# Decay scores of 13 of 32 head pairs moved from TensorE into VectorE's second operand, by a table in DRAM

## The chip, the cores and the metric

One core of one Trainium2 chip runs the whole program. The metric is device time in microseconds (us) of one execution. Engines are called PE (TensorE; PEld is its weight loads), DVE (VectorE), ACT (ScalarE), POOL (GpSimd) and SP (SyncE, which here only issues DMAs).

## The reference

For each of 8 batches and 8 heads, 576 positions and head dimension 64:

```
scores = q @ k.T / sqrt(64)
cum    = cumsum(log(clip(f, 1e-4, 1)))            # one row of 576 per head
decay  = cum[:, None] - cum[None, :]
scores = where(causal, scores + decay, -1e9)      # then softmax over keys
x      = softmax(scores) @ v                      # 8 heads side by side: 512 channels
gate   = sigmoid(conv over 5 positions of x, per channel)
out    = ((x @ w_val) * gate) @ w_out
```

The term `cum[:, None]` is the same for a whole row of scores and drops out of the softmax; what a kernel has to add is `-cum` of the key's position.

## The kernel before, in words

The work is cut into 32 pairs of heads (pair i is heads 2g and 2g+1 of batch i // 4). Two heads of 64 fill the 128 partitions. The 576 queries are nine blocks of 64; block j needs keys 0 to 64 j + 63. For a pair:

- **Scores** (`plan_s`). Three groups (`SG`, index u) of blocks: (8),(7); then (6,0),(2,4); then (1,3),(5). Each group takes one to three PSUM banks, and PE runs 64x64 tiles on all four quarters of its array. `decay` (before: 20 bf16 matmuls for each pair) adds the decays: its weights are a column of `pk`, a one-hot pattern repeated 64 times by a stride of zero, which picks three rows of `st`, the decays of many pairs as a sum of three bf16 parts. `prod` (20 fp32 matmuls, which the trace shows as 40 records) adds q times k. `mm` at line 233 is the helper that issues every matmul except the warm-up (line 352), so rows on line 233 are told apart by their tiles: `st,pk` is a decay, `Xr` a product, `U,vt` the attention times v (PV), `xh,wall` and `xl,wall` the w_val product (Mv), `hh` and `hl` the w_out product (Mo).
- **Softmax.** For each block DVE runs one custom instruction (line 423, `red`) that adds `mk` (zeros and, in the last 64 columns, the causal mask) to the scores in PSUM, scales them and keeps the row minimum in `negm`; ACT takes the exponential (line 427) into `P`, DVE transposes 32x32 blocks (line 462) into `T`, ACT or POOL copies half of it to `U` (line 248) and four DMAs (`U<-T`, line 260) carry the rest. Reciprocals of the sums travel by `zd` and `zb` through DRAM.
- **PV** writes x; a 5-tap convolution on POOL, ACT and DVE makes `gate`; x is split in `xh` and `xl` for Mv. After four pairs a batch's Mv and Mo can run.

At the start, f is loaded in two tables of 128 rows (21 pairs and 11 pairs, each row repeated up to three times). `logs` clips and takes the log, `decays` makes the running sum (line 337, a scan on DVE), its reference (line 339), the scaled values (line 341, ACT) and the three bf16 parts (`st`, by three casts at line 248 and two subtractions at line 345 in turn). Pair 0's products are issued ahead of its decays, since the decays come late. The weights w_val and w_out are decoded from 64-bit floats by lines 655 to 711 among the first pairs.

The order on every engine is fixed: each piece of work is a node of `Plan`, and `ORDER`, a compressed table of numbers, gives the sequence, the engine and the PSUM bank of each node. All DMAs go through SP's queue, one after another, but for the first two.

Of the kernel before, what the change touches and what calls it, by code (L numbers as in the profile page):

```python
# [793 lines left out]
```

## Time and profile before

| | us |
|---|---|
| median of three runs (439.27 to 442.82) | 439.31 |
| the profiled execution | 440.2 |
| its span, first to last instruction | 438.5 |
| PE busy in the span | 417.3 |
| DVE, ACT, POOL busy | 376.0, 335.5, 286.3 |

The span is 1.7 us shorter than the execution's own time; what lies around it is start and end of the program. All durations below are of this one execution, 0.9 us above the median. A group of PE rows is busy from the first start to the last end of its overlapping matmuls, so the cost of one kind of matmul is read from start to start: when the first of them begins, and when the next kind begins.

### The profile page before, as it was taken

The numbers are of one execution on the slowest core, as the hardware profiler recorded it, in microseconds if no ns is written. First come the engines' busy times: TensorE is split into PE (matmuls) and PEld (weight loads), VectorE is DVE, ScalarE is ACT, GpSimd is POOL, SyncE is SP. The second block draws the span as 40 slices with busy tenths as digits, with TensorE's granted clock in tenths as the row PEclk, the third lists the DMA queues.
The fourth block names the chain that finished last, engine by engine and source line by source line (L and its number), as shares of the span: only waits on it lengthen the run. The fifth ranks groups of instructions, "written<-read, shape, count | busy, mean of one in ns | idle before, by whom it ended". The sixth has DMA issues, their size and how long they took to land.

```text
span 438.5 us, 16745 instructions
## 1 busy us (share of the span) xinstructions
PE 417.3 (95%) x6640; PEld 356.5 (81%) x6640; DVE 376.0 (86%) x1045; ACT 335.5 (77%) x834; POOL 286.3 (65%) x296
## 2 busy tenths in 40 slices
PE   6768999999999999999999999899999999899996
PEld 5535788888898888898889789688889789799985
DVE  5999899899899898989989999598989879896840
ACT  5988899889779978877877888678778869682321
POOL 6576776687769686796367598769866864742200
PEclk9699999999999999999999999999999999999999
DMA  8679968976987886868678859886887757862112
GB/s 316 229 215 254 241 168 233 236 231 171 242 238 190 218 228 175 233 162 252 180 196 213 232 144 227 199 221 183 256 238 187 210 164 198 228 173 59 49 72 96
DMA packets 74847, 87.23 MB, mean 199 GB/s; under 512 B 48145, under 2 KB 48145, under 8 KB 74769
## 3 DMA queue, kind: packets, MB, share of 16 engines
q1 hardware_dynamic: 74480, 85.57, 70.9%
q8 instruction: 52, 0.85, 0.8%
q10 hardware_dynamic: 288, 0.59, 0.4%
q14 instruction: 27, 0.21, 0.2%
HBM read 52.29 MB, written 10.26 MB: 143 GB/s over the span
## 4 chain that ended last, share of the span: by engine, by line
PE 84%; DVE 6%; DMA 5%; issue 3%; SPq 1%; ACT 1%; POOL 0%; DVEq 0%; ACTq 0%; POOLq 0%
PE banks L233 84%; DVE banks L423 2%; DMA U<-T 2%; DVE T L462 2%; DMA sl<-in_w_out_dram 1%; DMA sh<-in_w_val_dram 1%; SPq L260 1%; DVE gate L345 0%; DVE negm L423 0%; DVE h L595 0%; DVE st L248 0%; DVE x L337 0%; POOL wall L711 0%; ACT ot L636 0%; DMA vt<-in_v_dram 0%
## 5 line engine op out<-in xcount | busy, mean ns | idle before, releaser
L427 ACT ACTIVATE P<-banks,negm 128x512 f32<-128x512 f32 (+8 forms) x288 | 149.6, 528 | 39.9 <-DVE negm L423 29.5
L423 DVE CUSTOM_DVE_ANT_0 banks<-banks,mk 128x512 f32<-128x512 f32 (+8 forms) x288 | 134.8, 506 | 16.3 <-PE banks L233 12.5
L564 POOL TENSOR_TENSOR gate<-gate,tm 128x576 f32<-128x576 f32 x77 | 109.5, 1424 | 46.8 <-DVE tm L255 11.0
L462 DVE STREAM_TRANSPOSE T<-P 128x1024 f32<-128x1024 f32 (+2 forms) x96 | 110.9, 1166 | 7.9 <-DMA U<-T 3.0
L233 PE MATMUL banks<-xh,wall 128*128 128x288 f32 x512 | 108.3, 298 | 0.0
L233 PE MATMUL banks<-Xr 64*64 64x288 f32 (+8 forms) x1280 | 104.2, 412 | 4.0 <-issue 2.8
L233 PEld LDWEIGHTS banks<-U,vt 64*64 64x64 f32 x3456 | 89.6, 133 | 6.8 <-ACT P L427 1.6
L233 PE MATMUL banks<-U,vt 64*64 64x128 f32 (+1 forms) x3456 | 91.0, 253 | 2.5 <-ACT P L427 1.0
L233 PE MATMUL banks<-wall,hh 128*128 128x512 f32 x288 | 90.5, 395 | 0.0
L233 PEld LDWEIGHTS banks<-xh,wall 128*128 128x128 f32 x512 | 83.6, 188 | 3.9 <-issue 0.9
L233 PEld LDWEIGHTS banks<-Xr 64*64 64x64 f32 x1280 | 65.0, 135 | 18.5 <-issue 9.4
L233 PE MATMUL banks<-xl,wall 128*128 128x288 f32 x256 | 75.5, 295 | 0.0
L248 ACT COPY U<-T 128x1440 f32<-128x1440 f32 x44 | 61.2, 1396 | 6.2 <-PE banks L233 3.2
L233 PEld LDWEIGHTS banks<-wall,hh 128*128 128x128 f32 x288 | 52.3, 188 | 12.0 <-issue 0.8
L427 ACT ACTIVATION_READ_ACCUMULATOR P<-banks,negm 128x1 f32 x288 | 58.4, 203 | 0.0
L233 PE MATMUL banks<-st,pk 64*64 64x256 bf16 (+8 forms) x640 | 47.8, 293 | 9.6 <-ACT P L427 6.1
L233 PE MATMUL banks<-wall,hl 128*128 128x512 f32 x144 | 56.2, 390 | 0.0
L233 PEld LDWEIGHTS banks<-xl,wall 128*128 128x128 f32 x256 | 48.1, 188 | 0.5
L233 PEld LDWEIGHTS <-pk 64*64 64x64 bf16 x640 | 27.7, 107 | 25.3 <-issue 20.4
L255 POOL TENSOR_SCALAR tm<-x,cw 128x576 f32<-128x576 f32 x36 | 27.7, 770 | 19.9 <-DVE gate L562 16.9
L423 DVE DVE_READ_ACCUMULATOR2_ANT negm<- 128x1 f32 x288 | 40.1, 139 | 0.0
L609 POOL TENSOR_TENSOR hl<-h,hh 128x576 fp32r<-128x576 f32 (+2 forms) x34 | 35.6, 1063 | 6.5 <-ACT tm L253 2.6
(103 smaller groups left out, 471.8 us busy)
## 6 DMA issues: line engine op xcount, KB each, us to landing
U<-T SPq DMA_DIRECT2D x128, 180.0 KB, 4.0
Xr<-in_x_dram SPq DMA_DIRECT2D x63, 288.0 KB, 5.0
vt<-in_v_dram SPq DMA_DIRECT2D x32, 320.0 KB, 5.0
out_dram<-ot SPq DMA_DIRECT2D x36, 256.0 KB, 3.6
vt<-in_v_dram SPq DMA_DIRECT2D x32, 256.0 KB, 5.5
zb<-zd SPq DMA_DIRECT2D x64, 80.0 KB, 4.0
zb<-zd SPq DMA_DIRECT2D x64, 64.0 KB, 3.6
sh<-in_w_val_dram SPq DMA_DIRECT2D x2, 512.0 KB
```

The costliest lines, as they stand in the source:

```text
L233: nc.tensor.matmul(out, lhsT=lhsT, rhs=rhs, start=start, stop=stop)
L248: (eng.copy if eng is nc.scalar else eng.tensor_copy)(out=out, in_=in_)
L255: eng.tensor_scalar(out=out, in0=in_, scalar1=col, scalar2=0.0, op0=ALU.mult, op1=ALU.add)
L260: lambda e: (nc.sync if e == "SP" else nc.scalar).dma_start(out=out, in_=in_), reads, writes, dma=span)
L423: nc.vector.tensor_tensor_reduce(out=sl, in0=sl, in1=mk[:, S - ext:], op0=ALU.add, op1=ALU.min, scale=-0.125, scalar=3.0e38, accum_out=neg ...
L427: nc.scalar.activation(out=dst, in_=bank(key)[:, a0:a0 + ext], func=AF.Exp, bias=negm[r][:, col], scale=-1.0, accum_out=zs[r][:, col])
L462: nc.vector.transpose(out=bass.AP(Tt.tensor, Tt.offset + 32 * FB[js[0]], [pitch, (32, nk), (CW, 2), (1, 32)]), in_=Pt[u])
L564: eng.tensor_tensor(out=gt, in0=gt, in1=to, op=ALU.add)
L609: eng.tensor_tensor(out=hl[jj][:, y:y + x1 - x0], in0=h2[jj % 2][:, x0:x1], in1=hh[jj][:, y:y + x1 - x0].bitcast(F32), op=ALU.subtract)
```

## The change

For 13 pairs, the odd ones from 7 to 31 (`TP`), PE runs no decay matmuls. The values of `-8 cum` are stored to DRAM (`lnf`), copied there into a table `tab` with every row eight times (three DMAs), and for each of the 13 pairs two DMAs of 128 x 576 floats bring the pair's rows, each to 64 partitions, into `dec` (two buffers). DVE's score instruction takes `dec` in place of `mk` as its second operand. The causal mask, which `mk` held, is then added on PE by 12 small bf16 matmuls a pair: an identity times a triangle, 64 or twice 64 columns each, behind the products.

Pair 0 takes its decays by fp32 matmuls straight from the scan's result (`cum`, with a one-hot column `p1` of -8), without the bf16 split. There is one f table in place of two (each pair once, and the first 16 pairs twice more), one log, one scan; the split runs for pairs 1 to 15 at the start and for 16 to 31 later, from `lnf`. The clearing of `mk` may go to DVE. `ORDER` is new.

```
-NS = (21, 11)
+NF = 16
+TP = tuple(range(7, 32, 2))
...
+        if i in TP:
+            for y in range(2):
+                load("dec", 1.4, i - 0.4 + 0.02 * y, dec[TP.index(i) % 2][:, y], bass.AP(tab.tensor, tab.offset + (24 * i + 8 * y) * S, [(S, 16), (0, 8), (1, S)]),
+                     [("tab", k) for k in range(3)], [("dec", TP.index(i) % 2, y)])
...
+    pool("start", 0.9, z + 3.27, mk_eyes, (), [("eyes",)])
+    any_("zero", {"POOL": 1.5, "DVE": 0.4}, z + 0.1, lambda eng: eng.memset(mk, 0.0), (), [("mk",)])
...
+                pick, row = (pk[hs, h, i:i + 1], st_) if i else (p1[hs], cum)
+                mm(bank(keys[y])[ps, at:at + e - a], pick.to_broadcast([D, D]), row[hs, a:e], start and fresh, last and stop)
...
+            def mask(h, half, item, start, stop, keys=keys):
+                y, js = item[:2]
+                hs, ps = slice(D * h, D * h + D), slice(D * half, D * half + D)
+                rhs = eyes[hs, 1]
+                to = bank(keys[y])[ps, (224 if js[0] == 8 else 0) + D * js[0]:]
+                gap = [(D * js[1] + D, 2)] if len(js) == 2 else []
+                mm(bass.AP(to.tensor, to.offset, [to.ap[0], *gap, (1, D)]), eyes[hs, 0],
+                   bass.AP(rhs.tensor, rhs.offset, [rhs.ap[0], *([(0, 2)] if gap else []), (1, D)]), False, stop)
...
-            if i:
-                pe("S", dur, p, lambda run=run, decay=decay, prod=prod: run((decay, prod)), ops + tab, keys, mode=1)
+            if late:
+                pe("S", (1.01, 0.9, 0.7)[u], p, lambda run=run, prod=prod, mask=mask: run((prod, mask)), ops + marks, keys, mode=1)
+            elif i:
+                pe("S", dur, p, lambda run=run, decay=decay, prod=prod: run((decay, prod)), ops + marks, keys, mode=1)
             else:
-                pe("S", dur, p, lambda run=run, prod=prod: run((prod,)), ops, keys, mode=1)
-                pe("Sd", 0.3, p, lambda run=run, decay=decay: run((lambda h, half, x, start: decay(h, half, x, False),)), tab, keys, mode=1)
+                pe("S", dur, p, lambda run=run, prod=prod: run((prod,), final=False), ops, keys, mode=1)
+                pe("Sd", (1.1, 1.0, 0.75)[u], p, lambda run=run, decay=decay: run((decay,), first=False), marks, keys, mode=1)
...
+                    in1 = dec[TP.index(i) % 2][:, y, 0:ext] if late else mk[:, S - ext:]
...
-                        nc.vector.tensor_tensor_reduce(out=sl, in0=sl, in1=mk[:, S - ext:], op0=ALU.add, op1=ALU.min, scale=-0.125,
+                        nc.vector.tensor_tensor_reduce(out=sl, in0=sl, in1=in1, op0=ALU.add, op1=ALU.min, scale=-0.125,
...
+        if not i:
+            load("lnf", 0.4, z + 1, lnf, val, kv, [("lnf",)], hold=0.48)
+            split(0, val, kv, z + 0.3)
+            for k in range(3):
+                load("tab", 1.6, z + 2 + 0.1 * k, bass.AP(tab.tensor, tab.offset + 8 * k * S, [(24 * S, NP), (S, 8), (1, S)]),
+                     bass.AP(lnf.tensor, lnf.offset + (0, D, 0)[k] * S, [(S, NP), (0, 8), (1, S)]), [("lnf",)], [("tab", k)])
```

In the rows below, numbers after a name tell its buffers apart (`Xr_76` and `Xr_80` both hold q and k of pair 7). On PE, the first scores of pair 7, first group. Before, the end of the decays and then the products:

```order
L233 LDWEIGHTS pk
L233 MATMUL banks<-st_70,pk 64x288
L233 LDWEIGHTS pk
L233 MATMUL banks<-st_70,pk 64x288
L233 MATMUL banks<-Xr_76 64x512 x2
L233 MATMUL banks<-Xr_76 64x288 x4
L233 LDWEIGHTS pk
L233 MATMUL banks<-st_70,pk 64x448
```

And now, the same group:

```order
L239 MATMUL banks<-Xr_80 64x288 x2
L239 MATMUL banks<-Xr_80 64x512 x2
L239 MATMUL banks<-Xr_80 64x288 x2
L239 LDWEIGHTS eyes
L239 MATMUL banks<-eyes 64x64
L239 LDWEIGHTS eyes
L239 MATMUL banks<-eyes 64x64
```

The six decays of up to 512 columns ahead of the products are gone, and four masks of 64 columns stand behind them.

On DVE, the start: from the scan to the first score instruction (ISA, with `banks` and `negm`). Before:

```order
L337 SCALAR_TENSOR_TENSOR x_100<-one,gate 128x576
L339 TENSOR_SCALAR ref_124<-x_100 128x1
L325 TENSOR_SCALAR tm<-tm 128x576
L248 CAST st_70<-gate 128x576
L345 SCALAR_TENSOR_TENSOR gate<-st_70,sel,gate 128x576
L248 CAST st_70<-gate 128x576
L345 SCALAR_TENSOR_TENSOR gate<-st_70,sel,gate 128x576
L248 CAST st_70<-gate 128x576
L703 TENSOR_SCALAR sh<-sh 128x512
L697 TENSOR_SCALAR sl<-sl 128x512
L703 TENSOR_SCALAR sl<-sl 128x512
L423 ISA banks,negm_89<-banks,mk 128x512
```

Now, from the operation ahead of the scan (the diagonal matrices of the first convolution, which POOL made before):

```order
L569 TENSOR_TENSOR tm<-ident,cw 128x640
L352 SCALAR_TENSOR_TENSOR x_104<-one,gate 128x576
L354 TENSOR_SCALAR ref<-x_104 128x1
L730 TENSOR_SCALAR sl<-sl 128x512
L736 TENSOR_SCALAR sl<-sl 128x512
L254 CAST st_70<-gate 128x576
L730 TENSOR_SCALAR sh<-sh 128x512
L736 TENSOR_SCALAR sh<-sh 128x512
L456 ISA banks,negm_93<-banks,mk 128x192
L456 ISA negm_93 128x1
L456 ISA banks,negm_93<-banks,mk 128x320
```

Two casts and both subtractions no longer stand ahead of pair 0's scores; seven score instructions of pair 0 are now ahead of the first subtraction, and the last cast of the split is on ACT, behind six exponentials of pair 0.

On SP, the DMAs behind the reciprocals (`zd_66`) of pair 4. Before:

```order
L260 DMA zd_66<-zt_95 4x32x32
L260 DMA zb_98<-zd_69 64x5x64 x2
L260 DMA zb_98<-zd_69 64x4x64 x2
L260 DMA U_84<-T_82 32x1440
L260 DMA Xr_76<-in_x_dram 128x576
L260 DMA zb_97<-zd_66 64x5x64
```

Now:

```order
L266 DMA zd_66<-zt_99 4x32x32
L266 DMA U_88<-T_86 32x1440
L266 DMA Xr_80<-in_x_dram 128x576
L266 DMA dec_73<-tab 128x1x576
L266 DMA zb_101<-zd_66 64x5x64 x2
L266 DMA ot<-in_w_out_dram 128x1024
```

A `dec` load, which pair 7's scores will need, has come between pair 4's transfers.

## Rows read from the trace of the kernel before

**Rows 1.** The page: busy engines, and the chain that ended last by engine.

```profile
PE 417.3 (95%) x6640; PEld 356.5 (81%) x6640; DVE 376.0 (86%) x1045; ACT 335.5 (77%) x834; POOL 286.3 (65%) x296
PE 84%; DVE 6%; DMA 5%; issue 3%; SPq 1%; ACT 1%; POOL 0%; DVEq 0%; ACTq 0%; POOLq 0%
```

**Rows 2.** Busy time by stretch: stretch, length, engines (x instructions), granted clock, DMA share, GB/s.

```profile
0.00:45.00 45.00, 31.20 (x421) 22.80 (x424) 39.30 (x121) 36.54 (x95) 29.15 (x56) 0.92 0.79 251
45.00:400.00 355.00, 351.31 (x6000) 303.38 (x5996) 317.12 (x886) 288.53 (x721) 254.25 (x238) 1.00 0.77 206
```

**Rows 3.** Timeline of PE, middle of the run: start, length, what, xcount.

```profile
188.53 0.36 PE L233 MATMUL banks<-st,pk 64*64 64x128 bf16 x6
188.72 0.81 PE L233 MATMUL banks<-Xr 64*64 64x128 f32 x12
189.37 0.41 PE L233 MATMUL banks<-st,pk 64*64 64x512 bf16 x6
189.59 1.16 PE L233 MATMUL banks<-Xr 64*64 64x512 f32 x12
...
197.81 0.46 PE L233 MATMUL banks<-st,pk 64*64 64x192 bf16 x7
198.03 0.57 PE L233 MATMUL banks<-Xr 64*64 64x192 f32 x3
```

**Rows 4.** Timeline of PE: two decays of 64 columns, and the next matmul.

```profile
193.32 0.19 PE L233 MATMUL banks<-st,pk 64*64 64x64 bf16 x2
193.35 0.57 PE L233 MATMUL banks<-Xr 64*64 64x448 f32 x4
```

**Rows 5.** Timeline of PE at the start, with the idle time ahead.

```profile
7.10 2.70 PE L233 MATMUL banks<-Xr 64*64 64x128 f32 x40 [1.16 <-DMA Xr<-in_x_dram]
12.47 0.81 PE L233 MATMUL banks<-st,pk 64*64 64x288 bf16 x20 [2.67 <-DVE st L248]
...
14.96 0.31 PE L233 MATMUL banks<-st,pk 64*64 64x128 bf16 x2 [0.62 <-ACT P L427]
```

**Rows 6.** Timeline of DVE at the start.

```profile
6.20 0.73 DVE L697 TENSOR_SCALAR sh<-sh 128x512 int32<-128x512 int32 x1 [0.72 <-DMA sh<-in_w_val_dram]
6.86 1.38 DVE L337 TENSOR_TENSOR_SCAN x<-one,gate 128x576 f32<-128x576 f32 x1
...
8.34 0.45 DVE L325 TENSOR_SCALAR tm<-tm 128x576 f32<-128x576 f32 x1
9.26 0.46 DVE L248 CAST st<-gate 128x576 bf16<-128x576 f32 x1 [0.47 <-ACT gate L341]
9.76 0.82 DVE L345 SCALAR_TENSOR_TENSOR gate<-st,sel,gate 128x576 f32<-128x576 bf16 x1
...
12.34 0.43 DVE L703 TENSOR_SCALAR sh<-sh 128x512 int32<-128x512 int32 x1
...
13.34 0.69 DVE L423 CUSTOM_DVE_ANT_0 banks<-banks,mk 128x512 f32<-128x512 f32 x1
```

**Rows 7.** Busy time by stretch at the start, columns as in rows 2.

```profile
13.20:20.10 6.90, 6.03 (x60) 4.47 (x58) 6.83 (x24) 6.72 (x21) 5.38 (x7) 0.51 0.70 236
```

**Rows 8.** DVE groups by line (the page, and with forms apart): xcount, busy, mean ns, idle before.

```profile
L423 DVE CUSTOM_DVE_ANT_0 banks<-banks,mk 128x512 f32<-128x512 f32 (+8 forms) x288 | 134.8, 506 | 16.3 <-PE banks L233 12.5
...
L528 DVE TENSOR_TENSOR xl<-x,xh 128x576 fp32r<-128x576 f32 x9 | 6.6, 753 | 0.3 <-ACT xh L248 0.2
```

**Rows 9.** DMA: SP's queue (packets, MB, share of 16 engines); one issue group's KB and landing.

```profile
q1 hardware_dynamic: 74480, 85.57, 70.9%
...
Xr<-in_x_dram SPq DMA_DIRECT2D x63, 288.0 KB, 5.0
```

**Rows 10.** The tile U: who waited for it (us, times), and its DMAs' time to landing.

```profile
PEld banks L233: 1.1, 2
PE banks L233: 0.7, 1
...
DMA to landing us min/median/max: 2.5/4.0/5.4
```

More of the change, by code (lines that the diff above doesn't have):

```diff
@@ L179, in tile_decay_attention_gated_mlp @@
     pk = const.tile([P, 2, NP], BF16, name="pk")
+    p1 = const.tile([P, 1], F32, name="p1")
     Xr = tiles(XB, [P, XW], F32, "Xr")
@@ L284, in mk_ident @@
                                 compare_op=ALU.is_equal, fill=0.0)
-    ref = [const.tile([P, 1], F32, name=f"ref{n}") for n in range(2)]
-    work = ((gate[2], x32[1][:, T0:], gate[0]), (tm[0], tm[1], tm[1]))
-    kws = (([("gate", 2)], [("x", 1, n) for n in range(3)], [("gate", 0)]), ([("tm", 0)], [("tm", 1)], [("tm", 1)]))
-    def load_f(n):
-        load("start", 0.75, z - 1 + n, work[n][0], f[n], (), kws[n][0], early=n == 0)
-    load_f(0)
+    ref = const.tile([P, 1], F32, name="ref")
+    ft, cum, val = gate[2], x32[1][:, T0:], gate[0]
+    kf, kc, kv = [("gate", 2)], [("x", 1, n) for n in range(3)], [("gate", 0)]
+    load("start", 0.75, z - 1, ft, f, (), kf, early=True)
     pool("start", 0.51, z, mk_ident, (), [("ident",)])
@@ L333, in decays, with mk_eyes @@
-    def decays(n):
-        (ft, cum, val), (kf, kc, kv) = work[n], kws[n]
-        p = z if n == 0 else NS[0] - 6.0
-        st_, ks = sts[n], [("st", n)]
-        dve("st0", 1.36, p, lambda: nc.vector.tensor_tensor_scan(out=cum, data0=one.to_broadcast([P, S]), data1=ft, initial=0.0, op0=ALU.mult, op1=ALU.add),
-            [*kf, ("one",)], kc)
-        dve("st0", 0.15, p, lambda: nc.vector.tensor_scalar(out=ref[n], in0=cum[:, S // 2:S // 2 + 1], scalar1=8.0, scalar2=0.0, op0=ALU.mult, op1=ALU.add),
-            kc, [("ref", n)])
-        act("st0", 0.76, p, lambda: nc.scalar.activation(out=val, in_=cum, func=AF.Identity, scale=-8.0, bias=ref[n]), [*kc, ("ref", n)], kv)
+    def mk_eyes():
+        nc.gpsimd.memset(eyes, 0.0)
+        for h in range(2):
+            for n, (op, fill) in enumerate(((ALU.not_equal, 1.0), (ALU.is_ge, -BIG))):
+                half = eyes[D * h:D * h + D, n]
+                nc.gpsimd.affine_select(out=half, in_=half, pattern=[[-1, D]], base=0, channel_multiplier=1, compare_op=op, fill=fill)
@@ L342, in decays, with split @@
+    act("st0", 0.76, z, lambda: nc.scalar.activation(out=val, in_=cum, func=AF.Identity, scale=-8.0, bias=ref), [*kc, ("ref",)], kv)
+    def split(n, val, kv, p):
+        st_, ks = sts[n], [("st", n)]
         for k in range(3):
@@ L717, in tile_decay_attention_gated_mlp @@
     for i in range(NP):
-        if i == NS[0] - 6:
-            load("lnf", 0.4, i, tm[0], lnf, [("lnf",)], kws[1][0], hold=0.48)
-            decays(1)
+        if i == NF - 6:
+            vb, kb = tm[0], [("tm", 0)]
+            for h in range(2):
+                load("lnf", 0.3, i, vb[D * h:D * h + D], bass.AP(lnf.tensor, lnf.offset + (D * h + NF) * S, [(0, 4), (S, NF), (1, S)]),
+                     [("lnf",)], kb, hold=0.48)
+            split(1, vb, kb, i)
         if i:
```

204 lines of the change are left out of this document (105 added, 99 removed).

## The prediction

> **What bounds the kernel now.** I read the page's busy line and chain first, then busy time by stretch, then the timelines of PE and DVE, then the DMA views. PE is busy 417.3 of 438.5 us and holds 84% of the chain [rows 1]. By stretch [rows 2] there are three parts. From 45 to 400 us PE is busy 351.31 of 355 us, so only 3.7 us are idle there; DVE has 317.12 (89%) and ACT 288.53 (81%). A microsecond of work taken from PE there shortens the run, unless DVE cannot feed PE that much sooner. From 0 to 45 us PE has 31.20 busy and 13.8 idle, while DVE is busy 39.30: DVE sets the pace of the start, since it has to bring the first four pairs through softmax, with the weights' decoding between them, before PE's other work exists. After 400 us only Mv and Mo of the last batches are left, which the change does not touch.
>
> **The decays taken from PE.** Each pair has 20 decay matmuls in three groups. From the start of a group's decays to the start of its products [rows 3]: 188.53 to 188.72 is 0.19 us, 189.37 to 189.59 is 0.22, 197.81 to 198.03 is 0.22. That is 0.63 us a pair, and the three groups have 5,760 columns together.
>
> In their place come 12 masks with 1,152 columns in all (six matmuls of 64 and six of 128). The trace has no masks. From below, by columns alone, they would take 1,152/5,760 of 0.63, that is 0.13 us. From above, if each cost as much as a decay of average size (0.63/20 = 0.032 us), 0.38 us. The nearest row is the pair of 64-column decays that start at 193.32, with the next matmul at 193.35 [rows 4]: 0.015 us each, so 12 take 0.18 us; I take 0.20, since half of them are twice as wide. So a pair saves 0.43 us (0.25 to 0.50), and 13 pairs save 5.6 us (3.3 to 6.5). It all lies on the path: the 13 pairs run between about 100 and 390 us, where PE has next to no idle time.
>
> The Trainium skill, page "TensorE: Matmul & The Clock Gate", section "Wait — 56ns, not 53.3ns?", speaks against part of this: start to start never drops below about 25 ns, however few columns. By that rule the masks would take 12 x 0.025 = 0.30 us and the 13 pairs would save 4.3 us; the two decays of rows 4, on different quarters of the array, came at 0.015 us each, which disagrees, so I keep the row.
>
> DVE's score instruction reads `dec` instead of `mk`: two operands of the same size and type from the same places. I take zero. It could only cost by waiting for the load, which is the last term.
>
> **The start.** Pair 0's decays wait today for the split: the products end at 9.80, and PE idles 2.67 us until the third cast is done [rows 5]. The split is three casts of 0.46 and two subtractions of 0.82 [rows 6], 3.0 us. Now pair 0's decays need the scan alone. As fp32 matmuls of the products' shapes they should take what those took, 2.70 us instead of 0.81 [rows 5]. The first group can start when the scan is done, about 8.3, or when PE is through with the products ahead of it, and it needs under 1.1 us (8 of 20 matmuls). So PE is ready with the first scores near 9.3 to 9.9.
>
> DVE then decides. Ahead of its scan now stand a clearing of `mk` and the diagonal (640 columns). Neither is in the trace on DVE; the nearest row is 0.753 us for 576 columns of a two-operand operation [rows 8], and the two together cost between 0.7 and 1.3 us. The wait of 0.72 us for the weights just ahead of the scan's neighbour [rows 6] no longer stands there and hides most of it. The scan therefore starts where it did, give or take 0.5 us. After it come the reference, four integer operations (the three ahead of the first score instruction take from 12.34 to 13.34, 0.33 each [rows 6]) and one cast: 1.4 + 0.2 + 1.3 + 0.5, with about half a microsecond of waiting for ACT's scaled values. The first score instruction starts near 10.5 instead of 13.34.
>
> That is not 2.8 us of gain. The other subtractions and casts move behind it, and pair 1 needs them. Two subtractions and one cast (2.1 us) plus eight score instructions (0.506 us on average [rows 8], 4 us) lie ahead of the last cast, which is now on ACT: pair 1's decays start near 16.6 where they started at 14.96 [rows 5]. There is a new wait as well: `val` is stored to `lnf` first, and the subtraction overwrites it, so it waits for that DMA. An `Xr` load of the same 288 KB takes 5.0 us to land [rows 9]; issued at about 9, it ends at 14, just when the subtraction's turn comes (10.5 plus 3.5 us for seven score instructions). Behind it on DVE stand the last two score instructions of pair 0 and its transposes. What is left is DVE's sum: out go a clip and a cast (0.45 and 0.46), and 1.2 us of waiting (0.72 and 0.47 in rows 6) is filled; in come 0.7 to 1.3 us. I take 1.0 us off the start. The bounds are 3.0 (all that the first score comes sooner is kept) and a loss of 2.0 (pair 1 is 1.6 us late, nothing is won back, and its first products follow later still).
>
> **The added DMA traffic.** SP's queue moved 85.57 MB in 70.9% of 438.5 us of all 16 engines, 3.63 us for each MB [rows 9]. 26 `dec` loads are 7.67 MB and take 27.8 us; three table copies of 0.59 MB take 6.4. One 288 KB load of f goes. Between 100 and 400 us that raises the DMA share of 0.77 [rows 2] by 0.09 to 0.86. PE waited for `U` 1.8 us in the whole run, in three waits, at a landing time of 4.0 us [rows 10], so most landings have room today. If landings stretch by about a tenth, a few more waits appear: I charge 0.8 us (0 to 10; the upper end is the last rival). SP issues 20 more DMAs of about half a microsecond each, over 300 us; its queue is not full.
>
> **Sum.** 440.2 for the profiled execution, minus 5.6, minus 1.0, plus 0.8, is 434.4. The median lies 0.9 below that execution, so I forecast 433.5 us.
>
> **The rivals.** One: *DVE gives half of it back.* From 45 to 400 us DVE is at 89%, and to do the same work in 5.6 us less it must reach 90.7%. For this speaks that PE's few waits are already on softmax results; against it, that DVE itself waits for PE. If half of the 5.6 returns as PE idle time and the start gives nothing, the time is 440.2 - 2.8 + 0.8 - 0.9 = 437.3.
>
> Two: *the start gets a second slow stretch.* PE's granted clock was half (1.2 instead of 2.4 GHz) from about 13.2 to 20.1 us [rows 7], after PE had idled 2.67 us up to 12.47 [rows 5]. Now it is busy there and idles later, from about 13.5 to 16.6, so the slow stretch may come when there is more to do. A slow stretch of 6.9 us costs at most half of it, 3.4 us, and today's cost nothing visible because DVE was busy throughout (6.83 of 6.90 [rows 7]). With 2.0 of that on the path and the 1.0 of the start lost: 433.5 + 1.0 + 2.0 = 436.5.
>
> Three: *the masks or the start do better.* Masks by columns alone and the whole 3.0 us of the start: 440.2 - 6.5 - 3.0 + 0 - 0.9 = 429.8.
>
> Four, on the other side: *the loads come in the way of `U`.* The DMA engines near nine tenths busy let the landing of `U<-T` grow from 4.0 us past what PV has as room. From the point where each of the 25 pairs from 7 on loses 0.27 us to it, the gain is gone (6.6/25). At 0.5 us for each, 12.5 us are lost, and the time is 440.2 - 6.6 + 12.5 - 0.9 = 445.2. For it speaks the share of 0.79 at the start [rows 2], which the changed kernel would exceed; against it, that PE waited only three times for `U`.
>
> **How the numbers follow.** The forecast has 0.58, with its own range of 431 to 436.5; rival one 0.15, two 0.07, three 0.10, four 0.10. A measurement of this kernel can tell about 1% from no change, 4.4 us, so "faster" is below 434.9. The forecast falls there in three cases of four (0.44), rival three always (0.10), the rest hardly (0.01): 0.55. Slower than 443.7 is rival four: 0.10. The rest, 0.35, is within 1%. The range from 429 to 440.5 leaves out most of rival four and little else.
>
> **What the profile of the changed kernel would show.** If right: PE busy near 412 us, a late pair's masks in 0.2 us from the first of them to the next kind, PE's idle time between 45 and 400 still under 6 us, the first score instruction on DVE between 10 and 11 us, PE's waits for `U` a few microseconds at most and DVE never long on `dec`. If wrong: PE's busy time down as said but its idle time up, with `DMA U<-T` as the releaser (rival four) or DVE's score instructions (rival one); a granted clock of one half later than 20 us (rival two); or masks at 0.3 us and more.

## The result, and the profile after

The changed kernel takes 443.64 us (median of 20 runs), the kernel before 440.55 in the same comparison: a ratio of 1.0056, interval 1.0032 to 1.0080. By the ratio it is slower by 2.5 us; 433.5 us was forecast, and 443.64 lies above the range that was given. The ratio leaves out the four of the changed kernel's runs that lie over 1.5% above its fastest one; the medians of all runs are 3.1 us apart. The profiled execution has a span of 440.7 us against 438.5.

The page of the changed kernel, busy engines and chain by engine [rows 1], then SP's queue [rows 9]:

```profile
PE 415.7 (94%) x6556; PEld 355.4 (81%) x6556; DVE 376.1 (85%) x1036; ACT 335.8 (76%) x840; POOL 284.6 (65%) x298
PE 55%; DMA 20%; DVE 10%; SPq 7%; ACT 3%; issue 3%; POOL 0%; DVEq 0%; ACTq 0%; POOLq 0%
q1 hardware_dynamic: 79032, 95.01, 80.6%
```

PE has only 1.6 us less to do, and its part of the chain has fallen from 84% to 55%: DMA and SP's queue together rise from 6% to 27%. A chain whose share moves from the busiest engine to the transfers says that the engine has begun to wait, even where its busy time fell.

Busy time by stretch, changed kernel [rows 2]; the last two are the stretches of half clock [rows 7]:

```profile
0.00:45.00 45.00, 33.82 (x427) 26.00 (x428) 37.84 (x116) 36.77 (x92) 23.41 (x57) 0.89 0.86 257
45.00:400.00 355.00, 344.89 (x5737) 296.37 (x5736) 315.27 (x876) 288.33 (x730) 256.46 (x238) 1.00 0.87 229
17.10:20.50 3.40, 3.40 (x36) 2.56 (x30) 3.40 (x6) 2.96 (x10) 2.30 (x7) 0.50 0.99 350
30.70:37.60 6.90, 5.47 (x122) 5.47 (x122) 4.35 (x19) 6.30 (x19) 3.84 (x3) 0.51 1.02 312
```

In the middle PE is now idle 355 - 344.89 = 10.1 us; it was 3.7. The work taken from PE has gone into waiting there. The DMA share went from 0.77 to 0.87, close to the 0.86 that was forecast from 100 us on.

Timeline of PE, changed kernel: masks of two late pairs and the matmul that follows them (start, length, what, xcount) [rows 3, 4]:

```profile
132.03 0.36 PE L239 MATMUL banks<-eyes 64*64 64x64 bf16 x4
132.32 0.40 PE L239 MATMUL banks<-xh,wall 128*128 128x288 f32 x1
...
183.30 0.26 PE L239 MATMUL banks<-eyes 64*64 64x128 bf16 x4
183.36 2.90 PE L239 MATMUL banks<-U,vt 64*64 64x128 f32 x106
...
186.96 0.20 PE L239 MATMUL banks<-eyes 64*64 64x64 bf16 x2
186.99 0.52 PE L239 MATMUL banks<-Xr 64*64 64x384 f32 x2
```

Ahead of other 64x64 tiles a mask takes 0.015 us (0.06/4 and 0.03/2), as the two decays of rows 4 did. Ahead of a 128x128 matmul four masks take 0.29 us, and the last of them about half of that (0.145 us, median of 14 such places in this trace). This should not be booked on the masks: in e12, which has none, the last product ahead of a 128x128 matmul is charged 0.31 us (median of 26).

Timeline of PE, then of DVE, at the start of the changed kernel [rows 5, 6]:

```profile
9.48 1.17 PE L239 MATMUL banks<-Xr 64*64 64x288 f32 x12
10.37 1.25 PE L239 MATMUL banks<-x,p 64*64 64x512 f32 x12
...
14.81 0.66 PE L368 MATMUL banks<-ident 128*128 128x128 f32 x4 [2.61 <-ACT P L460]
16.83 0.36 PE L239 MATMUL banks<-st,pk 64*64 64x128 bf16 x6 [1.36 <-ACT st L254]
```

```profile
6.44 1.35 DVE L352 TENSOR_TENSOR_SCAN x<-one,gate 128x576 f32<-128x576 f32 x1
...
9.97 0.35 DVE L456 CUSTOM_DVE_ANT_0 banks<-banks,mk 128x192 f32<-128x192 f32 x1
...
13.35 0.82 DVE L363 SCALAR_TENSOR_TENSOR gate<-st,sel,gate 128x576 f32<-128x576 bf16 x1 [0.33 <-DMA lnf<-gate]
```

The first score instruction starts at 9.97 (13.34 before), pair 1's decays at 16.83 (14.96 before). A lead of 3.4 us has become a lag of 1.9 within seven microseconds: the split now stands behind pair 0's scores. Pair 0's fp32 decays (`x,p`) took 1.54 us from 7.94 and 1.17 us from 10.37 to the next kind, 2.7 us as forecast, where the bf16 decays took 0.75 (12.47 to 13.22).

DVE's score instructions by operand, changed kernel [rows 8]:

```profile
L456 DVE CUSTOM_DVE_ANT_0 banks<-banks,mk 128x128 f32<-128x128 f32 (+8 forms) x171 | 80.1, 505 | 6.4 <-PE banks L239 4.9
L456 DVE CUSTOM_DVE_ANT_0 banks<-banks,dec 128x128 f32<-128x128 f32 (+8 forms) x117 | 55.2, 504 | 10.1 <-PE banks L239 6.5
```

504 ns from `dec`, 505 from `mk`: the other operand costs nothing. Most of the idle time ahead of either ends with PE, and no wait of DVE for a `dec` load is listed.

Waits for DMAs, changed kernel (who <- whom: us, times, longest) [rows 10], the last line from SP's own queue; then two places in PE's timeline; then a stretch of the chain that ended last (start, us, what):

```profile
DVE x L552 <- DMA zb<-zd: 6.9, 5, 2.4
PE banks L239 <- DMA zb<-zd: 2.0, 1, 2.0
PE banks L239 <- DMA Xr<-in_x_dram: 1.7, 2, 1.4
PE banks L239 <- DMA U<-T: 1.4, 1, 1.4
SPq L266 <- DMA dec<-tab: 5.4, 7, 1.2
```

```profile
32.16 5.08 PE L239 MATMUL banks<-U,vt 64*64 64x128 f32 x105 [1.43 <-DMA U<-T]
...
92.56 2.77 PE L239 MATMUL banks<-U,vt 64*64 64x128 f32 x106 [2.02 <-DMA zb<-zd]
```

```profile
81.92 0.22 DVE zt L473
82.14 0.02 issue
82.16 5.89 DMA zd<-zt
88.05 0.02 issue
88.07 0.02 SPq L266
88.09 0.03 issue
88.11 4.46 DMA zb<-zd
92.58 7.61 PE banks L239 x121
```

The reciprocals of a pair go out to DRAM (`zd`, 16 KB) and come back (`zb`), two DMAs in a row. Here they take 10.4 us, and PE idles 2.02 us ahead of PV at 92.56. PE's one wait for `U`, on which the forecast kept its eye, ends at 32.16, before the first `dec` load is issued (72.6 us).

The last line of the waits shows another way in which a load holds others up. SP issues in order, and it stood still until `dec` loads had landed, though nothing behind them on its queue needs their data. In this trace the DMAs share eight semaphores, and no semaphore has two transfers out at once: the next DMA on it is issued when the one before has landed. So a `zb` load was held until 151.27, when a `dec` load landed. More on this below, behind e20.

### The profile page after: what moved, and what is told of

Read it like the earlier page. It is cut to its first block, busy times and chain, and to the rows that moved or that the text cites. A ratio compares the mean times of both kernels' runs of the same rounds, so it can differ in the third digit from the quotient of the medians.

```text
span 440.7 us, 16603 instructions
## 1 busy us (share of the span) xinstructions
PE 415.7 (94%) x6556; PEld 355.4 (81%) x6556; DVE 376.1 (85%) x1036; ACT 335.8 (76%) x840; POOL 284.6 (65%) x298
## 3 DMA queue, kind: packets, MB, share of 16 engines
q1 hardware_dynamic: 79032, 95.01, 80.6%
## 4 chain that ended last, share of the span: by engine, by line
PE 55%; DMA 20%; DVE 10%; SPq 7%; ACT 3%; issue 3%; POOL 0%; DVEq 0%; ACTq 0%; POOLq 0%
PE banks L239 55%; SPq L266 7%; DVE banks L456 3%; DMA zd<-zt 3%; DMA zb<-zd 3%; DMA vt<-in_v_dram 3%; DVE T L495 3%; ACT P L460 2%; DMA tm<-lnf 2%; DMA U<-T 2%; DMA dec<-tab 2%; DMA Xr<-in_x_dram 2%; DMA sl<-in_w_out_dram 1%; DMA ot<-in_w_out_dram 1%; DMA lnf<-gate 1%
## 5 line engine op out<-in xcount | busy, mean ns | idle before, releaser
L460 ACT ACTIVATE P<-banks,negm 128x192 f32<-128x192 f32 (+8 forms) x288 | 149.7, 530 | 29.1 <-DVE negm L456 23.7
L495 DVE STREAM_TRANSPOSE T<-P 128x768 f32<-128x768 f32 (+2 forms) x96 | 111.0, 1167 | 2.8 <-ACT P L460 1.3
L239 PE MATMUL banks<-Xr 64*64 64x288 f32 (+8 forms) x1280 | 102.3, 416 | 1.9 <-DMA Xr<-in_x_dram 1.7
L456 DVE CUSTOM_DVE_ANT_0 banks<-banks,mk 128x128 f32<-128x128 f32 (+8 forms) x171 | 80.1, 505 | 6.4 <-PE banks L239 4.9
L239 PEld LDWEIGHTS banks<-Xr 64*64 64x64 f32 x1280 | 61.6, 135 | 17.1 <-issue 5.8
L456 DVE CUSTOM_DVE_ANT_0 banks<-banks,dec 128x128 f32<-128x128 f32 (+8 forms) x117 | 55.2, 504 | 10.1 <-PE banks L239 6.5
L254 ACT COPY U<-T 128x1440 f32<-128x1440 f32 x39 | 54.1, 1394 | 5.9 <-issue 3.9
L561 POOL TENSOR_TENSOR xl<-x,xh 128x576 fp32r<-128x576 f32 x25 | 35.7, 1429 | 14.9 <-ACT xh L254 5.1
L552 DVE TENSOR_TENSOR x<-banks,zb 128x256 f32<-128x256 f32 (+1 forms) x96 | 30.8, 347 | 15.3 <-PE banks L239 7.2
L254 POOL COPY U<-T 128x1440 f32<-128x1440 f32 x23 | 31.9, 1391 | 13.1 <-PE banks L239 8.5
```

The lines of the kernel that those rows point to most:

```text
L239: nc.tensor.matmul(out, lhsT=lhsT, rhs=rhs, start=start, stop=stop)
L254: (eng.copy if eng is nc.scalar else eng.tensor_copy)(out=out, in_=in_)
L456: nc.vector.tensor_tensor_reduce(out=sl, in0=sl, in1=in1, op0=ALU.add, op1=ALU.min, scale=-0.125, scalar=3.0e38, accum_out=negm[r][:, col])
L460: nc.scalar.activation(out=dst, in_=bank(key)[:, a0:a0 + ext], func=AF.Exp, bias=negm[r][:, col], scale=-1.0, accum_out=zs[r][:, col])
L495: nc.vector.transpose(out=bass.AP(Tt.tensor, Tt.offset + 32 * FB[js[0]], [pitch, (32, nk), (CW, 2), (1, 32)]), in_=Pt[u])
L552: nc.vector.tensor_tensor(out=bass.AP(to.tensor, to.offset, [to.ap[0], *dims, (1, D)]), in0=bank(keys[y])[:, D * first:D * last].rearrange ...
```

## The experiments

Three questions: what do the new order and start do without the rest; what is the relief of PE worth; what do the transfers cost. An edit `skip` keeps a node's place in the order and issues nothing. Only e3, e5, e6, e10, e13 and e14 add the right decays and masks to every pair; the others leave some out and serve for their time alone. Ratios are to the kernel before, run alongside, with 95% intervals. "Idle" is PE's idle time from 45 to 400 us, 355 less the busy time of that stretch; MB is what SP's queue moved.

Idle is read from one execution, which need not be a middle one: the profiles of e4 and e13 are of their shortest execution (436.68 us at a median of 442.73, and 438.69 at 443.19), that of e20 is of its longest (443.01 at 438.70). PE's busy time scatters too: after, e1, e2, e11 and e14 to e20 have the same work for PE, and their pages give 414.9 to 418.1 us.

| run | transfers added | ratio | interval | idle, us | MB |
|---|---|---|---|---|---|
| before | | 1 | | 3.7 | 85.57 |
| after | table, 26 loads | 1.0056 | 1.0032 to 1.0080 | 10.1 | 95.01 |
| e3, decays back on PE | none | 1.0026 | 0.9985 to 1.0068 | 1.9 | 85.57 |
| e5, decays back on PE | table, 26 loads | 1.0220 | 1.0143 to 1.0298 | 11.0 | 95.01 |
| e11 | none | 0.9921 | 0.9892 to 0.9951 | 4.8 | 85.57 |
| e12, no masks | none | 0.9896 | 0.9857 to 0.9936 | 6.1 | 85.57 |
| e4, no masks | table, 26 loads | 0.9998 | 0.9946 to 1.0049 | 6.1 | 95.01 |
| e15 | table | 0.9909 | 0.9869 to 0.9949 | 5.2 | 87.34 |
| e18 | 4 loads | 0.9938 | 0.9896 to 0.9980 | 5.4 | 86.75 |
| e20 | 13 loads | 0.9954 | 0.9922 to 0.9986 | 7.8 | 89.41 |
| e19 | 22 loads | 0.9982 | 0.9949 to 1.0016 | 6.7 | 92.06 |
| e17 | 26 loads | 1.0080 | 1.0050 to 1.0109 | 11.5 | 93.24 |
| e16 | table, 26 loads, unread | 1.0080 | 1.0037 to 1.0123 | 8.6 | 95.01 |
| e1 | table, 4 loads | 0.9999 | 0.9964 to 1.0033 | 6.4 | 88.52 |
| e2 | table, 4 loads, 22 tiny ones | 0.9982 | 0.9939 to 1.0026 | 6.6 | 88.62 |
| e14 | lean table, 26 loads | 1.0018 | 0.9984 to 1.0053 | 8.6 | 93.54 |
| e13, nine pairs | lean table, 18 loads | 1.0041 | 1.0016 to 1.0066 | 4.7 | 91.09 |

**Order and start alone (e3), and with the transfers (e5).**

```
-                     ... lambda run=run, prod=prod, mask=mask: run((prod, mask)), ...
+                     ... lambda run=run, prod=prod, decay=decay: run((decay, prod)), ...
-                    in1 = dec[TP.index(i) % 2][:, y, 0:ext] if late else mk[:, S - ext:]
+                    in1 = mk[:, S - ext:]
```

In e3 the `dec` and `tab` loads are `skip` as well; e5 keeps them, and nobody reads them.

> The changed kernel's order and start, with the decays of the 13 pairs back on PE as 20 bf16 matmuls ahead of the products, the mask back in mk, and no masks on PE, no table, no dec loads. Theory A: PE has some 3.6 us more work than with the loads gone (260 decays of 33 ns less 156 masks of 32 ns), so about 1.001 of before: the order as such costs nothing. Theory B: the order's waits stay and the work is added: 1.013.

> The changed kernel with the decays of the 13 pairs back on PE and no masks, as the run with the decays on PE (1.0026 of before), but with the table copies and all dec loads left in, which nobody reads now. Theory A1 (the traffic costs the same whatever PE does): 1.0026 plus the 0.006 that the loads cost in the changed kernel, about 1.009, with PE idle between 45 and 400 us near 6 to 8. Theory A2 (landings have room as long as PE still has the decays; the wait shows only because PE comes sooner): idle stays near 2 to 3, the time near 1.004.

The new order and start by themselves neither gain nor lose clear of noise (1.0026). The same with the transfers is 1.0220: 1.9%, some 8.5 us, for loads whose data no engine reads; both expectations for e5 were far below (1.009 and 1.004), and its interval is wide. In e5's profile part of it is a lower clock: stretches at half clock at 91.6 to 95.0 and 204.2 to 207.6, which e3 has not. They can explain at most half of their 6.8 us:

```profile
91.60:95.00 3.40, 3.12 (x66) 3.15 (x70) 0.89 (x2) 2.43 (x3) 2.15 (x2) 0.51 0.76 196
204.20:207.60 3.40, 3.26 (x8) 2.58 (x9) 2.09 (x5) 3.40 (x6) 2.53 (x5) 0.50 0.88 231
```

**Few or tiny loads (e1, e2), and no masks (e4).**

```
-                load("dec", ...
+                (load if i < 11 else skip)("dec", ...                              # e1
+                few = slice(0, P if i < 11 else 2)                                 # e2
+                load("dec", ..., dec[TP.index(i) % 2][few, y], ... [(S, 2), (1, S)]
+                ... lambda run=run, prod=prod: run((prod,)), ops + marks, ...      # e4
```

> The changed kernel with the dec loads of pairs 7 and 9 alone; the eleven later pairs read what those left in the two buffers (their decays are another pair's), so 22 loads of 288 KB are gone and every other instruction stands as it did. Theory A (the added traffic stretches landings, and PE waits for it): PE idle between 45 and 400 us falls from 10.1 to about 4, the time to about 0.993 of before. Theory B (the new order itself leaves PE waiting): idle stays near 10, time stays near 1.0056 of before.

> The changed kernel with all 26 dec loads issued, but from pair 11 on for 2 of 128 partitions only (other rows keep an older pair's decays): the issues on SP stay, the bytes go. Theory A with the bytes as the cause: as with the loads gone, about 0.993 of before. Theory A with SP's issue time and slots as the cause: at most a third of that gain, 1.003. Theory B: 1.0056.

> The changed kernel without the 12 mask matmuls of the 13 pairs (their diagonal blocks are not masked). The masks took 4.9 us from start to start. If PE's work sets the end, the time falls by 4 to 5 us, to about 0.995 of before. If the 13 pairs already wait for data (theories A or B where PE is not the bound), most of it turns into idle time: over 1.001.

e2 issues all 26 DMAs and still takes no longer than e1: the issues and their places on SP's queue are not the price, what they move is. Both lie between their expectations, nearer to the kernel before than to 0.993. e4 lies 0.6% below the change, between its two expectations, and the intervals meet; it decides nothing about the masks.

**The relief alone (e11), and without masks (e12); fewer pairs (e13) and a smaller table (e14).**

```
-                load("dec", ...
+                skip("dec", ...                                                     # e11, e12
-                load("tab", ...
+                skip("tab", ...                                                     # e11, e12
+                    in1 = mk[:, S - ext:]                                           # e11, e12
+                ... run((prod,)), ...                                               # e12
+                n = (S, 512)[y]                                                    # e13
+                (load if i >= 15 else skip)("dec", ..., dec[TP.index(i) % 2][:, y, 0:n], ...   # e13
+        late = i in TP and i >= 15                                                 # e13
```

e14 has `i >= 7` in the load, and `late` as in the change; both copy only the rows of their pairs into the table.

> The new order, start and masks, but without the table, its copies and the loads; the late pairs' score instruction reads the plain mask, so their decays are left out of the result. TensorE is thus relieved as in the change, and no transfer is added. Against the same order with the decays on TensorE (ratio 1.0026, work start to start 9.9 - 4.9 = about 3.7 to 5 us more) the theory that the added transfers are the whole price says: the relief is kept, ratio about 0.9945 (0.991 to 0.997), TensorE idle in 45-400 under 2.5 us. The theory that the relief runs into the softmax and into what feeds it says: idle of 4 to 5 us in 45-400 and a ratio near 0.999 to 1.002.

> The run before it, without the masks as well (they and the decays of the late pairs are left out of the result): TensorE is relieved of 0.7 us or so in each of 13 pairs, some 8.6 us. If TensorE alone bounds the order once the transfers are gone: ratio about 0.983 (0.979 to 0.988), idle in 45-400 under 3 us. If the relief is lost to what feeds TensorE: a ratio above 0.99, idle of 6 us or more.

> The change for the nine odd pairs from 15 on alone, the table holding their rows only and the second-half load only the 512 columns that are read. Pairs 7, 9, 11 and 13 keep decays on TensorE, so PV2 to PV15 have neither the table's copies nor the loads of the first half. If the price of the transfers falls in that first half (where after idles 4.5 and 4.0 us against 0.8 and 0): ratio 0.996 to 1.000. If each load costs wherever it stands: 1.003 to 1.006.

> The change as it is, with the table holding the rows of the 13 pairs only and the second-half loads cut to the 512 columns that are read, some 1.4 MB less of the 9.4 MB added. If the price goes with the bytes: 1.9% of loads less a seventh, a ratio near 1.003. If it is the number of loads or their places on the queue: 1.0056 as the change has it.

e11 decides most: without the transfers the change would have been 0.8% faster (0.5 to 1.1%). Busy lines of the page, e3, e11 and e12:

```profile
PE 421.1 (96%) x6660; PEld 358.4 (82%) x6660; DVE 376.9 (86%) x1036; ACT 335.9 (77%) x840; POOL 284.3 (65%) x298
```

```profile
PE 415.3 (96%) x6556; PEld 355.0 (82%) x6556; DVE 376.9 (87%) x1036; ACT 335.9 (77%) x840; POOL 284.6 (65%) x298
```

```profile
PE 413.1 (95%) x6400; PEld 350.2 (80%) x6400; DVE 376.4 (86%) x1036; ACT 335.3 (77%) x840; POOL 284.7 (65%) x298
```

From e3 to e11 PE loses 421.1 - 415.3 = 5.8 us of work, and the time 1.05%, 4.6 us: most of it is kept, though the intervals leave some 2 us open either way. e11's ratio is the one expected if the transfers were the whole price, its idle of 4.8 us the one expected if they were not. From e11 to e12 PE loses 2.2 us, 0.17 us a pair or 0.014 for each mask; with a scatter of 3 us between pages of equal work this is a rough figure, and from start to start the masks that don't stand ahead of a 128x128 matmul take 0.020 us each in the changed kernel. e12's idle of 6.1 us against e3's 1.9 fits some relief turning into waiting; by the ratios e12 is at 0.9896, between the two expectations. e13 fell at the upper of its two, so the price is not confined to the first half. e14 lies below the change, as expected by bytes, but the intervals meet.

In the same place where the changed kernel's chain runs through `zd` and `zb`, from 76 to 96 us, e11's chain is one piece:

```profile
75.98 20.23 PE banks L239 x318
```

**Which part of the transfers (e15, e16, e17).** e15 is e11 with the table's copies. e16 is the change with `in1 = mk[:, S - ext:]`, so that nobody waits for a load. e17 is e11 with the 26 loads taken from 16 rows of `lnf`, eight times each, in the same form.

> The order, start and masks of the change, with the three table copies of 0.59 MB and none of the loads; the late pairs' decays are left out of the result as in the run without either (ratio 0.9921, and 1.0056 with both: a price of 1.35%, some 6 us). If the price goes with bytes, the copies carry 1.77 of 9.44 MB, 0.25%: ratio about 0.995. If the copies weigh more because they stand at the start, where the four first pairs wait for transfers: 0.997 to 1.000, and most of the added idle time lies before PV7.

> The change with all its copies and loads, but VectorE's score instruction reads the plain mask instead of what was loaded, so no engine waits for a load; the late pairs' decays are left out of the result. If the price is the stretch of all other landings: 1.0056 as the change has it (1.002 to 1.008). If a good part of it is score instructions that wait for their own load: 0.995 to 1.000.

> The 26 loads without the table: each reads 16 rows eight times over, of the same size and form, from the values already stored in DRAM (other rows than the pair's), and no engine reads what they bring; the late pairs' decays are left out of the result. By bytes the loads carry 7.67 of 9.44 MB, four fifths of 1.35%: ratio about 1.003. If the table copies carry half of the price: about 0.999.

Busy time from 45 to 400 us, first e15, then e16, then e17 (PE first, DMA share last but one):

```profile
45.00:400.00 355.00, 349.85 (x5768) 300.73 (x5767) 319.13 (x886) 291.20 (x735) 260.24 (x242) 1.00 0.78 209
```

```profile
45.00:400.00 355.00, 346.38 (x5739) 296.33 (x5739) 315.47 (x876) 288.50 (x728) 256.01 (x239) 1.00 0.88 230
```

```profile
45.00:400.00 355.00, 343.55 (x5718) 294.22 (x5717) 312.28 (x870) 284.58 (x725) 253.16 (x236) 1.00 0.86 226
```

The table's copies cost nothing (0.9909), less than either expectation for e15. The loads alone cost all of it (1.0080), although no engine reads what they bring; that is more than either expectation for e17. Score instructions that wait for their own load are not the cause (e16 is no faster than the change). What is left is that the loads delay the other transfers.

**How many loads (e18, e19, e20).** e17 with four, the other 22, or every second of its loads: `(load if i < 11 else skip)`, `(load if i >= 11 else skip)`, `(load if y == 0 else skip)`.

> The run with the 26 loads alone (ratio 1.0080; none of them 0.9921), cut to the four loads of pairs 7 and 9; the late pairs' decays are left out of the result. If each load costs the same (1.6% over 26): 0.9945 (0.992 to 0.997). If the first ones, which land while the zd and zb transfers of pairs 3 to 5 are under way, weigh most: 0.998 to 1.001, as the two runs with the change's table and few full loads (0.9982 and 0.9999) have it.

> The same, with the 22 loads of pairs 11 to 31 and not the first four; the late pairs' decays are left out of the result. If each load costs the same: 1.0055. If the first four carry half of the price: 1.000 or less.

> The same, with one load of the two for every late pair, 13 loads of 0.295 MB spread over the whole run; the late pairs' decays are left out of the result. If the price goes with the bytes: half of 1.6%, a ratio of 1.000. If it sets in only as the queues fill up: 0.994 to 0.997. If one load in the way of a pair's transfers costs as much as two: 1.004 or more.

The price rises with the number: 0, 4, 13, 22 and 26 loads give 0.9921, 0.9938, 0.9954, 0.9982 and 1.0080. The first four points lie within their intervals of 0.03% a load. The step from 22 to 26 is larger than that: e18 agrees with equal prices, e19 with half of the price in the first four loads, e20 with a price that sets in late. Whether the price grows faster than the number near the full load, or four loads in an early place weigh more when the others follow, these runs do not settle; e1 and e2 (0.9999 and 0.9982), above e15 and e18, also hint at something that the count alone does not give.

One count in the traces rises with the price, and has the step from 22 to 26 loads too. SP waited until an earlier DMA had landed, leaving out `zd` (whose landing `zb` needs), for 6.8 us in 12 waits in e11, 5.4 in e15, 6.5 in e18, 14.5 in e20, 15.5 in e19, 22.6 in 40 waits in e17, 24.3 in e16 and 19.4 in the changed kernel. All that stands behind such a wait on the queue comes later. Whether this is how the price is paid, or longer landings are, was not tested; the same loads on another engine's queue, with semaphores of their own, would tell.

**No table at all (e6, e9, e10).** `dec` is read straight from `lnf`, each row 64 times, for all 13 pairs (e6), for pairs 7 and 9 only (e9), or from pair 15 on (e10). The first half of a pair's decays comes by the load shown, the other half by two loads of 64 rows:

```
+                        nc.sync.dma_start(out=to[:, 0], in_=bass.AP(lnf.tensor, lnf.offset + i * S, [(D * S, 2), (0, D), (1, S)]))
```

> The changed kernel without the table: the three copies are gone, and each dec half is loaded straight from lnf, one row read 64 times (three DMAs a pair, 13 more issues in all). In the changed kernel pairs 2 to 7 took 61.3 us from PV to PV where the run with decays on PE, without copies or loads, took 57.8. If the copies are the cause of that, pairs 2 to 7 fall below 59.5 us and the time to about 1.000 of before. If reading one row 64 times is slow, dec lands later than 7 us and DVE waits on it: 1.006 and more. If neither, 1.0056 as it was.

> The same without the table, and with dec loads for pairs 7 and 9 alone (later pairs read an old pair's decays): next to none of the added traffic is left, PE keeps its relief. If traffic is all that turned the gain into idle time, PE idle between 45 and 400 us is near 2, as with the decays on PE, PE's work is 3.6 us less than there, and the time is 0.994 of before. If the relief by itself runs into softmax, idle stays at 4 to 5 us and the time near 0.999.

> The changed kernel with the decays on DVE for the nine odd pairs from 15 on alone, loaded straight from lnf, no table; pairs 7 to 13 have their decays on PE. Where the two runs with the same order differ, pairs 2 to 7 and 11 to 15 lost 3.5 and 3.6 us by the change, and pairs 15 to 31 won 1.7. If the losses are bound to the crowded first half, this one keeps the win: about 0.998 to 0.999 of before, better than the run with all decays on PE (1.0026). If the loads cost wherever they are: 1.004.

e6 is at 1.1125 (1.1073 to 1.1177), e10 at 1.0798 (1.0752 to 1.0845), e9 at 1.0037 (1.0002 to 1.0072). These loads are slow in themselves, so e9 and e10 say nothing of what they were made for. By e6's trace, a load of 128 rows from two rows of DRAM lands 10.1 us after the end of its issue (median of 13; 8.6 to 11.4) where one from the table, 16 rows eight times each, takes 4.6 in the changed kernel. In e6 the waits for it stand in the view of waits:

```profile
PE banks L239 <- DMA Xr<-in_x_dram: 13.2, 5, 4.4
DVE banks L467 <- DMA dec<-lnf: 12.8, 3, 5.8
```

Of the versions that leave nothing out, none beat the kernel before; e14, at 1.0018, comes nearest.

## Why the prediction was wrong

**The decays taken from PE: right.** 5.6 us were forecast, 5.8 measured in PE's work (e3 to e11; with the scatter of equal work 3.0 to 6.2) and 4.6 of the time, by ratios of 0.3 to 0.4% uncertainty. The masks, the unknown of this term, were taken at 0.20 us a pair and cost 0.17 (e11 to e12) to 0.24 (start to start). The Trainium skill, page "TensorE: Matmul & The Clock Gate", section "Wait — 56ns, not 53.3ns?", with about 25 ns from start to start would have given 0.30 us; 0.015 us in the timeline and 0.014 from e12 disagree for these 64x64 tiles, and the row that the forecast kept was the better guide. The average over all masks from start to start, 0.030 us, would have misled: it books the wait ahead of a 128x128 matmul on whichever tile stands last.

**DVE's operand: right**, zero. **The start: its steps right, its sum not.** The first score instruction was forecast near 10.5 and came at 9.97, pair 1's decays near 16.6 and came at 16.83, the new wait for `lnf` was there with 0.33 us. Of the 1.0 us off the start nothing is seen: e3, which has all of it, is at 1.0026 (0.9985 to 1.0068), about 1.1 us slower. The sum counted DVE alone and left out PE's side. PE's work in e3 is 3.8 us above the kernel before. Pair 0's fp32 decays are 2.0 of it (2.7 against 0.75). The clock can be up to 1.7: until 45 us e3 and the changed kernel have 10.2 us at half clock and the kernel before 6.9; the second stretch in the changed kernel, 30.7 to 37.6 us, comes behind an idle time of 2.27 us. By this estimate the earlier start pays for it and no more, and it is also why PE is busy 415.7 us and not 412; no run takes the two apart.

**The step that failed is "I charge 0.8 us" for the added traffic.** The runs show 1.0056 - 0.9921 = 1.35%, 5.9 us, and e16 and e17 7.0. With 4.6 for 5.6 and 1.1 lost for 1.0 gained, this makes the 2.5 us by which the kernel is slower. The DMA share (0.87) was right, and so was the stretch: from e11 to the changed kernel the mean time from the end of an issue to the landing grows by 7 to 11% (`U` 3.86 to 4.28 us, `Xr` 4.51 to 4.83, `zb` with four blocks 3.41 to 3.78, with five 3.21 to 3.52, `zd` 2.66 to 2.95), the tenth that was forecast.

What was wrong is the price of that tenth. The forecast read it from PE's waits for `U` alone, 1.8 us in all; those are 1.8 us in the changed kernel too (1.4 on PE, 0.4 on its weight loads). The price appeared elsewhere: `zd` and `zb` stand one after another on the way to PV's result, as from 76 to 96 us; DVE's waits for `zb` are 6.9 us (1.0 in e11); and SP waits for landings before it issues more. PE, with 3.7 us idle in 355, had no room. That these make up the whole price is argued: only 3.4 of PE's 10.1 us idle end directly with a DMA, 1.9 us of it lie before the first `dec` load (1.6 us in e11), and in e17, where the price is higher, PE waits 3.7 us for `U` and DVE never for `zb`. Which transfers are late differs from version to version.

SP issues 30 more DMAs (493 against 463), not 20; by e2 this has no large part in it.

**The rivals.** Four came true in its price: it named 0.27 us for each of 25 pairs as the point where the gain is gone, and 5.9/25 is 0.24, against a gain of 0.8% instead of its 6.6 us. Its sign, PE's idle time ending with `U`, is missing in the changed kernel, and there in e17 (1.28 us at 110.04, 1.35 at 269.89). Its chance of 0.10 had no row behind it: the 10 us that the forecast itself set as the upper end of this term stood beside 0.8 without a row that chose between them. One was partly so: idle rises by 2.8 us from e3 to e11 without any transfer. Two's sign came, a half clock later than 20 us; its price was not isolated, and with the same start e11 has 3.4 us of it there, e12 none. Three did not come: neither the masks by columns alone nor its start.

## What to carry to other kernels

A transfer that no engine waits for need not be free when the busiest engine is 99% busy and its inputs come by chains of DMAs: here 7.7 MB of such loads cost 7 us, about 0.9 us for each MB, a quarter of the 3.7 us that a MB occupies 16 DMA engines. It is no fixed price: 6.5 MB, 22 of the 26 loads, cost 2.7 us. Before a change that trades compute for traffic, list all DMAs in series on the path (here `zd`, `zb`, `U`, `Xr`), not only the one that is waited for today, price a stretch of each, and look at what the issuing queue itself waits for. The cheapest test of such a trade is two kernels: the relief without the transfer, and the transfer without the relief.

## What the runs showed that was not expected

The form of a load decided more here than its bytes: 288 KB from two DRAM rows, 64 times each, lands in 10.1 us and from 16 rows, eight times each, in 4.6; with 13 pairs of the former the kernel is 11% slower while SP's queue moves less (93.24 MB against 95.01). Reading a row 64 times is not slow by itself: the two other loads of each pair in e6 do that too, from one row to 64 partitions each, and land in 4.0 and 4.2 us (medians). The trace shows a difference in the landing. The semaphore of every slow load is updated three times, once about 1.0 us after the start of its issue and twice near its end, and that of the others 16 times. This fits a load whose data went by two of the 16 DMA engines, one for each of its two source rows; a run with another outer count would show it, and there is none.

A wait of about two microseconds on PE can be paid twice. In e11 PE idles 1.93 us until 183.19, and its clock is granted at half, 1.2 GHz, from 184.0 us on:

```profile
183.19 0.40 PE L239 MATMUL banks<-xh,wall 128*128 128x288 f32 x1 [1.93 <-DVE x L556]
```

```profile
184.00:187.40 3.40, 3.40 (x16) 3.40 (x16) 3.37 (x15) 3.32 (x8) 0.63 (x1) 0.50 0.87 192
```

In the changed kernel the wait of 2.02 us ahead of 92.56 had no such effect, so it is not the length of the wait alone.
